# Moving the first weight conversion and the first large product in the hand-written order of an attention and feed-forward kernel

## Chip, core and metric

The kernel runs on one core of a Trainium2 chip. The metric is the device time of one execution in microseconds. Before the change three runs took 835.82, 836.37 and 837.70 us, so the median is 836.37 us.

## What is computed

The reference is windowed attention followed by a gated feed-forward layer.

```python
# q, k, v: (8 batches, 8 heads, 576 tokens, 64); x: 4608 tokens x 512
scores = (q @ k.T) / 8          # heads 0-3: the last 32 keys; heads 4-7: every 4th key of the last 128
attn   = softmax(where(mask, scores, -1e9))
x      = (attn @ v) -> 4608 x 512
h      = x @ w_in               # 512 x 2048
out    = (h * clip(h + 3, 0, 6) / 6) @ w_out   # 2048 x 512
```

## The kernel before, in words

**Attention.** The attention is cut into 48 trios; a trio is half of one batch for one of the two mask kinds. The first twelve trios are written out by hand in the table ORDER (lines 57 to 79), where each name is one step on one engine and its number is the trio. For a trio t the steps follow each other like this:

- `k`, `v` load keys with queries, and values (SP issues the transfer, L195 and L204).
- `B` is a block on PE: the mask by one product (L337), 48 score products of 64x32 (L227), and between them 48 value products (L237) of an older trio. FOLLOW says which one: block 2 carries the values of trio 0, 3 of 1, 4 of 2, 5 of 3, 7 of 5, 8 of 6, 9 of 7, 10 of 8, 11 of 9. `V` is a block with values alone.
- `R` is the maximum on DVE (L264), `S` the subtraction on DVE (L268), `X` the exponent on ACT (L291).
- `E` is the transposition on PE (L354, three products), `CA` its copy to SBUF on ACT (L367). The values' products of the trio need `CA`.
- `Z` divides by the sums on DVE (L312, L313, L315), `Y` transposes on PE (L354), `CX` copies on ACT (L371).
- `XH` rounds the tokens to the high part on ACT (L447), `XL` makes the low part on DVE (L453).

**Weights.** `w` loads one 512 KB piece of the weights (L484). It is split into a high and a low part by `Q` and `U` on ACT (L503, L499), `s`, `j` and `a` on DVE (L507, L513, L520), `h` on ACT (L523) and `l` on DVE (L529). Even pieces are w_in, odd ones w_out.

**Feed-forward.** `G` is a large product on PE, twelve matmuls of 128x384 (L545 to L547). `RE` on ACT (L553), `T` on DVE (L556), `GH` on ACT (L560) and `GL` on DVE (L564) apply the gate and split the result. `H` is the second product, nine matmuls of 128x512 (L595 to L597). After ORDER ends, a planner (`_in_time`) sets the order of all later work; it does not read ORDER.

**What sets the order.** Every engine runs its steps strictly in the order in which ORDER names them, and so does SP with the transfers. A name such as `w0@R1` means that the issue of w0 also waits until R1 is done. A step that waits therefore holds everything behind it on its engine. PE writes to two pools of PSUM banks: `ps_h` with two banks for `G`, and `ps_a` with six for all else, taken in turn.

The loop that reads the table:

```python
for name in ORDER.split():
    name, _, behind = name.partition("@")
    kind = name.rstrip("0123456789")
    issued[name] = first_operations[kind](int(name[len(kind) :]))
    if behind:
        tc.add_manual_dep(issued[name].ins, issued[behind].ins.name, ...)
```

Of the kernel before, what the change touches and what calls it, by code (L numbers as in the profile page):

```python
# [54 lines left out]

FOLLOW = {2: 0, 3: 1, 4: 2, 5: 3, 7: 5, 8: 6, 9: 7, 10: 8, 11: 9}
ORDER = """
k0 M0 M1 k1 k2 v0 k3 v1 B0 k4 v2 R0 S0 B1 X0 R1 E0 S1 w0@R1 CA0 X1 k6@X1 B2 Z0 R2 E1 CA1 Y0 k5@CA1 B3 S2 CX0 XH0 v3@S2
X2 XL0 v4@XL0 Q0 U0 E2 s0 Z1 CA2 B4 R3 j0 S3 w2@j0 a0 X3 v5@a0 h0 Y1 Z2 B6 CX1 XH1 R4 Y2 R6 E3 CX2 XL1 k7@CX2 CA3 S6
XH2 B5 S4 X6 w4@XH2 XL2 X4 Q2 l0 E6 U2 Z3 E4 v6@E6 CA6 R5 CA4 Y3 k8@CA6 s2 V4 CX3 S5 XH3 j2 X5 XL3 Q4 E5 Z4 U4 CA5 a2  # L60
Y4 B7 s4 CX4 w6@a2 j4 h2 XH4 l2 k9@j4 B8 Z5 R7 v7@R7 Y5 XL4 CX5 Z6 G0 XH5 S7 Q6 w7@Q6 R8 X7 w1@X7 XL5 Y6 U6 S8 E7 G1
CX6 a4 k10@a4 CA7 s6 v8@CA7 XH6 j6 X8 h4 XL6 B9 w5@G1 RE0 a6 RE1 l4 h6 k11@RE1 T0 E8 Q7 Z7 G2 CA8 GH0 R9 Q1 v9@GH0 GL0
U1 S9 U7 Y7 T1 B10 X9 s1 CX7 l6 GH1 v10@CX7 j1 XH7 E9 G3 R10 RE2 CA9 XL7 Q5 S10 U5 Z8 B11 X10 RE3 a1 GL1 h1 E10 T2 Y8
CA10 Z9 CX8 V10 GH2 R11 XH8 Y9 l1 CX9 Z10 H0 XH9 XL8 XL9 w3@XL8 S11 Y10 G8 GL2 CX10 w16@S11 w13@S11 T3 X11 s5 XH10 s7
GH3 XL10 E11 RE8 GL3 G6 CA11 j5 U3 w28@CA11 T8 Q3 a5 GH8 G10 j7 RE6 w11@GH8 h5 GL8 U16 T6 l5 Q16 Q13 G4 s16 GH6 a7
RE10 Q28 j16 v11@a7 h7 T10 H2 w8@j16 Q11 a16 U28 l7 h16 s3 H3 s28 GH10 GL6 l16 RE4 j3 Q8 w30@RE4 V11 U8 T4 GL10 GH4
G20 w17@U8 Z11 GL4 w9@Z11 a3 Y11 s8 RE20 G13 j28 CX11 h3 T20 XH11 j8 Q30 H4 XL11 U30 l3 w29@Q30 GH20 a8 Q17 a28 U17 H1
GL20 RE13 s17 h8 T13 Q9 j17 GH13 H8 U9 l8 w31@GH20 h28 GL13 Q31 a17 U31 G12 s9 l28 h17 Q29 j9 U29 l17 w14@GL20 G25 Q14
a9 RE12 s31 h9 s30 T12 U14 H20 l9 RE25 s14 GH12 T25 GL12 G5 w15@T25 j14 GH25 j31 GL25 a14 H13 RE5 a31 h14 T5 Q15 l14
U15 H12 j30 GH5 h31 s15 GL5 j15 G18 l31 w23@j14 Q23 a15 a30 h15 G11 s29 RE18 l15 h30 T18 l30 w18@U15 GH18 H10 j29 RE11  # L70
GL18 T11 a29 Q18 G27 GH11 U18 GL11 h29 s18 H18 l29 w19@T18 Q19 RE27 j18 U19 T27 a18 GH27 H25 s19 h18 GL27 l18 w10@Q18
Q10 U10 j19 H11 U11 s10 a19 s11 h19 j10 G22 l19 w12@a19 j11 a10 G15 RE22 a11 h10 T22 h11 l10 GH22 H6 l11 w20@j10 Q12
RE15 GL22 Q20 T15 U20 G14 GH15 s20 U12 GL15 j20 U13 s12 H22 RE14 a20 T14 h20 s13 GH14 l20 w21@l11 G7 Q21 GL14 U21 j13
j12 G24 a13 RE7 a12 h13 T7 h12 l13 w22@l20 H14 GH7 RE24 l12 GL7 T24 G17 s21 Q22 j21 GH24 U22 GL24 a21 U23 G16 RE17 s22
s23 h21 T17 j22 GH17 G9 l21 w24@l12 Q24 a22 U24 j23 h22 H24 s24 l22 j24 w25@l22 a23 H15 RE16 GL17 h23 a24 RE9 T16 h24
l23 G26 GH16 T9 Q25 GL16 U25 l24 w27@GH16 GH9 s25 G19 j25 a25 H17 h25 Q27 l25 H16 RE26 GL9 w26@H17 k12 k13 v12 v13 M2
RE19 T26 T19 G21 GH26 GH19 Q26 H9 U26 s26 U27 j26 H7 RE21 GL26 a26 T21 h26 GL19 H5 GH21 l26 GL21 s27 j27 G23 a27 h27
H21 l27 RE23 T23 GH23 H19 GL23 H23
"""


# [1466 lines left out]
```

## Time and profile before

| what | value |
|---|---|
| median of three runs | 836.37 us |
| the profiled execution's own time | 839.36 us |
| its span, first to last instruction | 837.5 us |
| PE busy in the span | 825.6 us |
| DVE busy | 646.5 us |
| ACT busy | 574.0 us |
| mean granted PE clock | 0.990 |

The profiled execution took 2.99 us longer than the median, and 1.9 us of it lie outside the span. Times in the traces count from the start of the span. A view by windows gives for each stretch of time how long each engine was busy, how many instructions it ran (x), and the granted clock of PE, where 1.00 is full speed. A timeline row gives start and duration, the engine (PEld is the weight load that goes with a PE product), the line, the tiles, and in brackets the idle time before it and what ended that. Matmuls overlap, so their durations are longer than the distance from one start to the next.

### The profile page before, as it was taken

The page shows a single profiled execution, that of the slowest core. Times are in us where ns is not written, and L with a number is a line of the kernel's source. Part 1 is how long each engine was busy: PE and PEld are TensorE (multiplying, and loading weights), DVE is VectorE, ACT ScalarE, POOL GpSimd, SP SyncE. Part 2 cuts the span into 40 slices and gives each one's busy share as a digit, 9 for nine tenths or more (in the row PEclk, how much of TensorE's full clock was granted, in tenths as well). Part 3 has the DMA queues.
Part 4 walks back from the last instruction along what each step waited for, and adds up shares of the span by engine and source line. Part 5 has one row for each costly group of instructions (what it writes and reads, how often), then busy time and mean ns, then how long its engine had stood idle before and what let it go on. Part 6 is the DMA issues. An engine that isn't in the chain of part 4 may idle for free.

```text
span 837.5 us, 22133 instructions
## 1 busy us (share of the span) xinstructions
PE 825.6 (99%) x8756; PEld 777.4 (93%) x8756; DVE 646.5 (77%) x1313; ACT 574.0 (69%) x1400; POOL 55.5 (7%) x114
## 2 busy tenths in 40 slices
PE   6999999999999999999999999999999999999998
PEld 4788999898888888999999999999999999999998
DVE  4899997646777988898898677888686798445983
ACT  3688775334799885799975698855698755455552
POOL 0000000011122212000300001000001000000000
PEclk9699999999999999999999999999999999999999
DMA  7668433242778999899997798886788866996381
GB/s 287 195 214 272 126 102 114 92 171 93 247 237 270 295 356 352 297 387 394 389 329 266 262 324 306 315 298 238 281 300 309 273 230 227 335 367 222 131 295 58
DMA packets 115783, 214.70 MB, mean 256 GB/s; under 512 B 7520, under 2 KB 40288, under 8 KB 115680
## 3 DMA queue, kind: packets, MB, share of 16 engines
q1 hardware_dynamic: 115680, 213.29, 73.3%
q8 instruction: 69, 1.13, 0.5%
q14 instruction: 34, 0.28, 0.1%
HBM read 174.47 MB, written 38.80 MB: 255 GB/s over the span
## 4 chain that ended last, share of the span: by engine, by line
PE 97%; DMA 1%; DVE 1%; ACT 0%; issue 0%; SPq 0%
PE ps_o L745 28%; PE ps_x L754 10%; PE ps_x L756 9%; PE ps_x L755 9%; PE ps_h L545 6%; PE ps_h L546 5%; PE ps_h L547 5%; PE ps_o L595 5%; PE ps_o L597 5%; PE ps_o L596 5%; PE ps_b L245 2%; PE ps_b L227 1%; PE ps_a L227 1%; PE ps_a L245 1%; PE ps_a L237 1%; PE ps_a L354 1%
## 5 line engine op out<-in xcount | busy, mean ns | idle before, releaser
L745 PE MATMUL ps_o<-gh,ring 128*128 128x384 f32 x896 | 230.8, 334 | 0.0
L745 PEld LDWEIGHTS ps_o<-gh,ring 128*128 128x128 f32 x896 | 162.0, 188 | 0.0
L745 PE MATMUL ps_o<-gl,ring 128*128 128x384 f32 x448 | 149.7, 334 | 0.0
L1208 DVE TENSOR_TENSOR gl<-g,gh 128x384 fp32r<-128x384 f32 x224 | 116.2, 553 | 27.9 <-ACT gh L1204 26.5
L1204 ACT CAST gh<-g 128x384 fp32r<-128x384 f32 x224 | 104.3, 513 | 31.2 <-PE ps_o L745 23.6
L754 PE MATMUL ps_x<-x,ring 128*128 128x384 f32 x256 | 88.4, 345 | 0.0
L545 PE MATMUL ps_h<-x,wi 128*128 128x384 f32 x256 | 88.0, 344 | 0.0
L546 PE MATMUL ps_h<-x,wi 128*128 128x384 f32 x256 | 86.2, 337 | 0.0
L755 PE MATMUL ps_x<-x,ring 128*128 128x384 f32 x256 | 86.1, 336 | 0.0
L756 PE MATMUL ps_x<-x,ring 128*128 128x384 f32 x256 | 86.1, 336 | 0.0
L547 PE MATMUL ps_h<-x,wi 128*128 128x384 f32 x256 | 86.1, 336 | 0.0
L745 PEld LDWEIGHTS ps_o<-gl,ring 128*128 128x128 f32 x448 | 84.1, 188 | 0.1
L595 PE MATMUL ps_o<-wo,gh 128*128 128x512 f32 x192 | 74.9, 390 | 0.0
L596 PE MATMUL ps_o<-wo,gh 128*128 128x512 f32 x192 | 74.7, 389 | 0.0
L597 PE MATMUL ps_o<-wo,gl 128*128 128x512 f32 x192 | 74.7, 389 | 0.0
L553 ACT ACTIVATE t<-ps_h,three 128x384 f32<-128x384 f32 x64 | 37.1, 582 | 50.6 <-PE ps_h L547 50.5
L756 PE MATMUL ps_x<-cell,ring 128*128 128x384 f32 x192 | 64.9, 338 | 0.0
L755 PE MATMUL ps_x<-cell,ring 128*128 128x384 f32 x192 | 64.7, 337 | 0.0
L754 PE MATMUL ps_x<-cell,ring 128*128 128x384 f32 x192 | 64.7, 337 | 0.0
L1173 DVE TENSOR_TENSOR g<-g 128x768 f32<-128x768 f32 x64 | 60.8, 951 | 0.0
L556 DVE SCALAR_TENSOR_TENSOR t<-t,ps_h 128x384 f32<-128x384 f32 x64 | 35.1, 550 | 28.6 <-ACT t L553 27.9
L1058 DVE TENSOR_TENSOR s<-ps_x,s 128x384 f32<-128x384 f32 x64 | 35.3, 552 | 25.3 <-ACT s L1051 24.6
(112 smaller groups left out, 1767.6 us busy)
## 6 DMA issues: line engine op xcount, KB each, us to landing
ring<-sums SPq DMA_DIRECT2D x112, 512.0 KB, 8.3
ring<-rights SPq DMA_DIRECT2D x112, 512.0 KB, 7.2
st<-in_w SPq DMA_DIRECT2D x32, 512.0 KB, 4.3
kq<-in_qk SPq DMA_DIRECT2D x39, 416.0 KB, 5.1
v<-in_v SPq DMA_DIRECT2D x39, 390.0 KB, 5.6
sums<-wi SPq DMA_DIRECT2D x24, 256.0 KB, 6.5
rights<-wo SPq DMA_DIRECT2D x24, 256.0 KB, 5.4
out<-o SPq DMA_DIRECT2D x15, 384.0 KB, 2.8
```

What stands on the lines that cost most here:

```text
L545: nc.tensor.matmul(ph, lhsT=wt(f, 0)[:, ks], rhs=a, start=(kt == 0), stop=False)
L546: nc.tensor.matmul(ph, lhsT=wt(f, 0)[:, ks], rhs=b, start=False, stop=False)
L547: ins = nc.tensor.matmul(ph, lhsT=wt(f, 1)[:, ks], rhs=a, start=False, stop=(kt == NK - 1))
L595: nc.tensor.matmul(po[c][tt], lhsT=gh[:, rows], rhs=wt(f, 2), start=first, stop=False)
L596: nc.tensor.matmul(po[c][tt], lhsT=gh[:, rows], rhs=wt(f, 3), start=False, stop=False)
L597: return nc.tensor.matmul(po[c][tt], lhsT=gl[:, rows], rhs=wt(f, 2), start=False, stop=(f == NF - 1))
L745: nc.tensor.matmul(banks[part][:, :CH], lhsT=right[:, a, cols], rhs=x, start=(start and not i), stop=(i == 2), skip_group_check=True)
L754: nc.tensor.matmul(bank, lhsT=tile_[:, 0, ks], rhs=h[:, kt], start=(start and kt == 0), stop=False, skip_group_check=True)
L755: nc.tensor.matmul(bank, lhsT=tile_[:, 0, ks], rhs=l[:, kt], start=False, stop=False, skip_group_check=True)
L756: nc.tensor.matmul(bank, lhsT=tile_[:, 1, ks], rhs=h[:, kt], start=False, stop=(kt == 1), skip_group_check=True)
L1204: nc.scalar.copy(two[0], gated_tile(g, q, k))
L1208: nc.vector.tensor_tensor(out=two[1], in0=gated_tile(g, q, k), in1=two[0].bitcast(F32), op=ALU.subtract)
```

## The change

Only the table ORDER changes. Its first 18 names and its last 417 of 588 stay as they are; the 153 between are the same names in another order, and 13 of the transfers among them wait for another step than before. No instruction is added or taken away.

```diff
-k0 M0 M1 k1 k2 v0 k3 v1 B0 k4 v2 R0 S0 B1 X0 R1 E0 S1 w0@R1 CA0 X1 k6@X1 B2 Z0 R2 E1 CA1 Y0 k5@CA1 B3 S2 CX0 XH0 v3@S2
-X2 XL0 v4@XL0 Q0 U0 E2 s0 Z1 CA2 B4 R3 j0 S3 w2@j0 a0 X3 v5@a0 h0 Y1 Z2 B6 CX1 XH1 R4 Y2 R6 E3 CX2 XL1 k7@CX2 CA3 S6
...
-Y4 B7 s4 CX4 w6@a2 j4 h2 XH4 l2 k9@j4 B8 Z5 R7 v7@R7 Y5 XL4 CX5 Z6 G0 XH5 S7 Q6 w7@Q6 R8 X7 w1@X7 XL5 Y6 U6 S8 E7 G1
...
+k0 M0 M1 k1 k2 v0 k3 v1 B0 k4 v2 R0 S0 B1 X0 R1 E0 S1 CA0 X1 w0@X1 B2 Z0 R2 E1 CA1 k6@CA1 Y0 B3 S2 CX0 k5@S2 XH0 X2
+XL0 v3@XL0 E2 CA2 Z1 R3 v4@R3 B4 S3 Q0 X3 U0 s0 j0 w2@j0 Y1 CX1 a0 v5@a0 h0 Z2 B6 XH1 R4 Y2 R6 E3 CX2 XL1 k7@CX2 CA3
...
+k9@Z4 U4 CA5 a2 Y4 s4 j4 B7 CX4 h2 XH4 l2 XL4 w6@XL4 G0 a4 R7 h4 S7 RE0 X7 Z5 B8 l4 E7 v8@X7 Y5 CA7 T0 CX5 G1 R8 XH5
+Q6 XL5 S8 X8 Z6 Y6 CX6 U6 k10@XL5 w7@Q6 B9 RE1 XH6 s6 E8 T1 j6 CA8 XL6 w1@Z6 a6 G2 h6 R9 Q7 S9 l6 w5@G2 X9 Z7 k11@a6
```

There are two places. On ACT, near the first weight conversion, the rows are Q0 (L503), U0 (L499), CA2 (L367), X3 (L291), h0 (L523) and CX1 (L371); the difference reads:

```order
-L503 ACTIVATE va<-st 128x512
-L499 ACTIVATE va<-st 128x512
-L367 COPY a<-ps_a 128x384
-L291 ACTIVATE e<-e 128x384
-L523 CAST wi<-va 128x512
-L371 COPY xf<-ps_a 128x6x2x32
+L367 COPY a<-ps_a 128x384
+L503 ACTIVATE va<-st 128x512
+L291 ACTIVATE e<-e 128x384
+L499 ACTIVATE va<-st 128x512
+L371 COPY xf<-ps_a 128x6x2x32
+L523 CAST wi<-va 128x512
```

CA2 now stands ahead of Q0, and X3 between Q0 and U0; on DVE, R3 and S3 likewise stand ahead of s0 and j0.

On PE, behind block 7, the first large product G0 (L545 to L547) now comes at once; these are its first rows:

```order
 L237 MATMUL ps_a<-first,a 32x65
 L227 MATMUL ps_a<-first 32x64
+L545 MATMUL ps_h<-x_78,wi 128x384
+L546 MATMUL ps_h<-x_84,wi 128x384
+L547 MATMUL ps_h<-x_78,wi 128x384
```

PE's order there was block 7, block 8, Y5, G0, Y6, E7, G1, block 9; it is now block 7, G0, block 8, E7, Y5, G1, Y6, block 9.

On DVE, the followers of block 8 stood like this before: Z6 (three rows), S7, R8, XL5 (L453), S8, then a4, s6, j6 of the weights:

```order
L312 TENSOR_SCALAR z<-ps_a 128x6
L313 RECIPROCAL z<-z 128x6
L315 TENSOR_TENSOR x<-ps_a,z 128x384
L268 TENSOR_TENSOR e<-ps_a,mx 128x384
L264 TENSOR_REDUCE mx<-ps_a 128x6
L453 TENSOR_TENSOR x_86<-xf,x_80 128x2x192
L268 TENSOR_TENSOR e<-ps_a,mx 128x384
L520 ISA va<-va 128x1024
L507 TENSOR_SCALAR va<-va 128x512
L513 SCALAR_TENSOR_TENSOR va<-st,va 128x512
```

Now R8, XL5 and S8 stand ahead of Z6, and T1 (L556) stands between s6 and j6:

```order
L264 TENSOR_REDUCE mx<-ps_a 128x6
L453 TENSOR_TENSOR x_86<-xf,x_80 128x2x192
L268 TENSOR_TENSOR e<-ps_a,mx 128x384
L312 TENSOR_SCALAR z<-ps_a 128x6
L313 RECIPROCAL z<-z 128x6
L315 TENSOR_TENSOR x<-ps_a,z 128x384
L507 TENSOR_SCALAR va<-va 128x512
L556 SCALAR_TENSOR_TENSOR t<-t,ps_h 128x384
L513 SCALAR_TENSOR_TENSOR va<-st,va 128x512
```

Z6 moved behind XL5. Further on, DVE's order is XL6, a6, R9, S9, l6, Z7, GL0, s1, j1, where it was XL6, a6, l4, T0, Z7, R9, GL0, S9, T1, s1, l6, j1.

More of the change, by code (lines that the diff above doesn't have):

```diff
@@ L57 @@
 ORDER = """
-k0 M0 M1 k1 k2 v0 k3 v1 B0 k4 v2 R0 S0 B1 X0 R1 E0 S1 w0@R1 CA0 X1 k6@X1 B2 Z0 R2 E1 CA1 Y0 k5@CA1 B3 S2 CX0 XH0 v3@S2
-X2 XL0 v4@XL0 Q0 U0 E2 s0 Z1 CA2 B4 R3 j0 S3 w2@j0 a0 X3 v5@a0 h0 Y1 Z2 B6 CX1 XH1 R4 Y2 R6 E3 CX2 XL1 k7@CX2 CA3 S6
-XH2 B5 S4 X6 w4@XH2 XL2 X4 Q2 l0 E6 U2 Z3 E4 v6@E6 CA6 R5 CA4 Y3 k8@CA6 s2 V4 CX3 S5 XH3 j2 X5 XL3 Q4 E5 Z4 U4 CA5 a2
-Y4 B7 s4 CX4 w6@a2 j4 h2 XH4 l2 k9@j4 B8 Z5 R7 v7@R7 Y5 XL4 CX5 Z6 G0 XH5 S7 Q6 w7@Q6 R8 X7 w1@X7 XL5 Y6 U6 S8 E7 G1
-CX6 a4 k10@a4 CA7 s6 v8@CA7 XH6 j6 X8 h4 XL6 B9 w5@G1 RE0 a6 RE1 l4 h6 k11@RE1 T0 E8 Q7 Z7 G2 CA8 GH0 R9 Q1 v9@GH0 GL0
@@ L63 @@
[L63 to L77, printed above, removed]
@@ L78 @@
-H21 l27 RE23 T23 GH23 H19 GL23 H23
+k0 M0 M1 k1 k2 v0 k3 v1 B0 k4 v2 R0 S0 B1 X0 R1 E0 S1 CA0 X1 w0@X1 B2 Z0 R2 E1 CA1 k6@CA1 Y0 B3 S2 CX0 k5@S2 XH0 X2
+XL0 v3@XL0 E2 CA2 Z1 R3 v4@R3 B4 S3 Q0 X3 U0 s0 j0 w2@j0 Y1 CX1 a0 v5@a0 h0 Z2 B6 XH1 R4 Y2 R6 E3 CX2 XL1 k7@CX2 CA3
+S6 XH2 B5 S4 X6 w4@XH2 XL2 X4 Q2 l0 E6 U2 Z3 E4 v6@E6 CA6 R5 CA4 Y3 k8@CA6 s2 V4 CX3 S5 XH3 j2 X5 XL3 v7@XL3 Q4 E5 Z4
+k9@Z4 U4 CA5 a2 Y4 s4 j4 B7 CX4 h2 XH4 l2 XL4 w6@XL4 G0 a4 R7 h4 S7 RE0 X7 Z5 B8 l4 E7 v8@X7 Y5 CA7 T0 CX5 G1 R8 XH5
@@ new lines @@
+Q6 XL5 S8 X8 Z6 Y6 CX6 U6 k10@XL5 w7@Q6 B9 RE1 XH6 s6 E8 T1 j6 CA8 XL6 w1@Z6 a6 G2 h6 R9 Q7 S9 l6 w5@G2 X9 Z7 k11@a6
+Y7 Q1 CX7 B10 U1 U7 GH0 v9@GH0 GL0 s1 GH1 v10@CX7 j1 XH7 E9 G3 R10 RE2 CA9 XL7 Q5 S10 U5 Z8 B11 X10 RE3 a1 GL1 h1 E10
+T2 Y8 CA10 Z9 CX8 V10 GH2 R11 XH8 Y9 l1 CX9 Z10 H0 XH9 XL8 XL9 w3@XL8 S11 Y10 G8 GL2 CX10 w16@S11 w13@S11 T3 X11 s5
+XH10 s7 GH3 XL10 E11 RE8 GL3 G6 CA11 j5 U3 w28@CA11 T8 Q3 a5 GH8 G10 j7 RE6 w11@GH8 h5 GL8 U16 T6 l5 Q16 Q13 G4 s16
+GH6 a7 RE10 Q28 j16 v11@a7 h7 T10 H2 w8@j16 Q11 a16 U28 l7 h16 s3 H3 s28 GH10 GL6 l16 RE4 j3 Q8 w30@RE4 V11 U8 T4 GL10
@@ new lines @@
+GH4 G20 w17@U8 Z11 GL4 w9@Z11 a3 Y11 s8 RE20 G13 j28 CX11 h3 T20 XH11 j8 Q30 H4 XL11 U30 l3 w29@Q30 GH20 a8 Q17 a28
+U17 H1 GL20 RE13 s17 h8 T13 Q9 j17 GH13 H8 U9 l8 w31@GH20 h28 GL13 Q31 a17 U31 G12 s9 l28 h17 Q29 j9 U29 l17 w14@GL20
+G25 Q14 a9 RE12 s31 h9 s30 T12 U14 H20 l9 RE25 s14 GH12 T25 GL12 G5 w15@T25 j14 GH25 j31 GL25 a14 H13 RE5 a31 h14 T5
+Q15 l14 U15 H12 j30 GH5 h31 s15 GL5 j15 G18 l31 w23@j14 Q23 a15 a30 h15 G11 s29 RE18 l15 h30 T18 l30 w18@U15 GH18 H10
+j29 RE11 GL18 T11 a29 Q18 G27 GH11 U18 GL11 h29 s18 H18 l29 w19@T18 Q19 RE27 j18 U19 T27 a18 GH27 H25 s19 h18 GL27 l18
@@ new lines @@
+w10@Q18 Q10 U10 j19 H11 U11 s10 a19 s11 h19 j10 G22 l19 w12@a19 j11 a10 G15 RE22 a11 h10 T22 h11 l10 GH22 H6 l11
+w20@j10 Q12 RE15 GL22 Q20 T15 U20 G14 GH15 s20 U12 GL15 j20 U13 s12 H22 RE14 a20 T14 h20 s13 GH14 l20 w21@l11 G7 Q21
+GL14 U21 j13 j12 G24 a13 RE7 a12 h13 T7 h12 l13 w22@l20 H14 GH7 RE24 l12 GL7 T24 G17 s21 Q22 j21 GH24 U22 GL24 a21 U23
+G16 RE17 s22 s23 h21 T17 j22 GH17 G9 l21 w24@l12 Q24 a22 U24 j23 h22 H24 s24 l22 j24 w25@l22 a23 H15 RE16 GL17 h23 a24
+RE9 T16 h24 l23 G26 GH16 T9 Q25 GL16 U25 l24 w27@GH16 GH9 s25 G19 j25 a25 H17 h25 Q27 l25 H16 RE26 GL9 w26@H17 k12 k13
@@ L79 @@
+v12 v13 M2 RE19 T26 T19 G21 GH26 GH19 Q26 H9 U26 s26 U27 j26 H7 RE21 GL26 a26 T21 h26 GL19 H5 GH21 l26 GL21 s27 j27
+G23 a27 h27 H21 l27 RE23 T23 GH23 H19 GL23 H23
 """
```

## The prediction

> **What bounds the kernel now.** First the page: span, PE's share, and the chain that ended last.
>
> ```profile
> span 837.5 us, 22133 instructions
> PE 825.6 (99%) x8756; PEld 777.4 (93%) x8756; DVE 646.5 (77%) x1313; ACT 574.0 (69%) x1400; POOL 55.5 (7%) x114
> q8 instruction: 69, 1.13, 0.5%
> PE 97%; DMA 1%; DVE 1%; ACT 0%; issue 0%; SPq 0%
> ```
>
> PE bounds it: it idles for 11.9 us in all. The view by windows says when.
>
> ```profile
> 58.40:837.00 778.60, 775.56 (x7512) 738.48 (x7510) 604.29 (x1210) 538.05 (x1319) 54.88 (x108) 1.00 0.74 258
> ```
>
> From 58.4 us on PE idles for 3.0 us in 778.6, at full clock. The change ends before that point, and all later work keeps its order, so whatever first moves the second product H0 (56.04 us) moves the end by as much. The question is how long PE needs to reach H0. Two things delay it there. One is the clock, in windows of 3.41 us, at whose edges it changes:
>
> ```profile
> 7.97:11.38 3.41, 2.49 (x103) 1.74 (x101) 1.61 (x6) 1.38 (x3) 0.00 (x0) 1.00 1.01 391
> 14.79:18.21 3.42, 0.62 (x36) 0.47 (x36) 1.56 (x5) 1.58 (x3) 0.00 (x0) 1.00 0.79 297
> 28.45:31.86 3.41, 1.90 (x55) 1.28 (x54) 3.32 (x10) 3.38 (x9) 0.00 (x0) 1.00 0.84 268
> 31.86:35.27 3.41, 3.41 (x101) 2.31 (x101) 2.29 (x6) 1.91 (x6) 0.00 (x0) 0.50 0.62 193
> 35.27:38.69 3.42, 3.42 (x102) 3.18 (x102) 3.24 (x10) 0.40 (x1) 0.00 (x0) 0.50 0.68 218
> ```
>
> The columns are length, busy time of PE, PEld, DVE, ACT and POOL, clock, DMA share, GB/s. After a window with 0.62 us of PE work, and after one with 1.90, the clock is half; after 2.49 it stayed whole. The other is the wait in block 4, in the chain that ended last (start, length, what):
>
> ```profile
> 8.06 7.26 DMA st<-in_w
> 15.34 0.66 ACT va L503
> 16.55 0.38 ACT a L367
> 16.98 0.24 PE ps_a L237
> 17.55 1.02 issue
> ```
>
> The load of w0 ends at 15.32, Q0 (L503) waits for it, U0 and then CA2 (L367) stand behind it, and block 4's values start at 16.98. Then PE waits for another 1.02 us, and no semaphore is named. The same happened one block earlier (the other two rows are the end of E2 and block 4's mask):
>
> ```profile
> 12.79 0.21 PE L237 MATMUL ps_a<-first,a 64*32 64x65 f32 x1 [0.22 <-issue]
> 14.19 0.38 PE L354 MATMUL ps_a<-ident,e 128*128 128x128 f32 x2
> 14.51 0.33 PE L337 MATMUL ps_a<-mi 32*128 32x384 bf16 x1
> ```
>
> Between the stop that ends at 12.79 and the one that ends at 18.57 the timeline has 127 matmuls (88 of block 3, 3 transposes, 36 of block 4), with a weight load each: 254 instructions. The page's 17,512 PE instructions over its 69 instruction loads are 254 too. I read both stops as PE waiting for the next piece of its code, while the data loads fill the DMA engines (share 1.01 in the window 7.97:11.38).
>
> **First part: CA2 and R3 ahead of the conversion.** E2 ends at about 14.57, so CA2 can run at 14.65 and block 4's values start at 15.2 instead of 16.98: 1.78 us earlier. But after 36 matmuls, some 0.4 us, PE needs the same piece of code. Up to block 4's mask (14.51) nothing on PE changes, and w0 is only issued some 1.2 us later into a queue that is full anyway, so the piece should arrive at the same 18.57. Then block 4 ends where it did, the window 14.79 to 18.21 again holds some 0.6 us of PE work, and the clock halves as before. The bounds are 0 (the piece comes when it came) and 1.78 us (its wait vanishes); I take 0, since the code load is what ended last in that row. R3, S3 and Z1 come earlier, which nothing uses: PE's next steps, Y1 and block 6, stand behind block 4. The transfers of k6, k5, v3 and v4 are issued one step later each, behind a queue that still has work, for blocks that start after 20 us: nothing.
>
> The Trainium skill, "Runtime: NRT & Kernel Launch", section "Instruction fetch mechanics", has PE's code streamed in blocks of 256 instructions, the crossing "mostly hidden". The block's size agrees with the 254; the 1.02 us does not agree with hidden. By that page this part would gain the 1.78 us.
>
> **Second part: G0 ahead of block 8.** The PE rows from here on, before:
>
> ```profile
> 32.48 0.49 PE L337 MATMUL ps_a<-mi 32*128 32x384 bf16 x1
> 34.91 0.50 PE L337 MATMUL ps_a<-mi 32*128 32x384 bf16 x1
> 40.45 0.49 PE L354 MATMUL ps_a<-ident,x 128*128 128x128 f32 x3
> 41.02 0.42 PE L545 MATMUL ps_h<-x,wi 128*128 128x384 f32 x1
> 43.30 0.33 PE L337 MATMUL ps_a<-mi 32*128 32x384 bf16 x1
> 44.89 0.55 PE L354 MATMUL ps_a<-ident,e 128*128 128x128 f32 x3
> 56.04 0.47 PE L595 MATMUL ps_o<-wo,gh 128*128 128x512 f32 x1
> ```
>
> They are block 7, block 8, Y6, G1, block 9, E8 and H0. A large product takes about 2.1 us at full clock (2.28 from G1 to block 9, with the change of operand), a block 1.59 (43.30 to 44.89). DVE's and ACT's costs, each from one start to the next, come from these rows: on DVE Z7 (45.00 to 45.89: 0.89), R9, GL0, S9, T1, s1, l6, and j1 in the last:
>
> ```profile
> 45.00 0.16 DVE L312 TENSOR_SCALAR z<-ps_a 128x6 f32<-128x6 f32 x1 [0.49 <-PE ps_a L237]
> 45.89 0.55 DVE L264 TENSOR_REDUCE mx<-ps_a 128x6 f32<-128x384 f32 x1
> 46.40 0.56 DVE L564 TENSOR_TENSOR gl<-t,gh 128x384 fp32r<-128x384 f32 x1
> 46.88 0.55 DVE L268 TENSOR_TENSOR e<-ps_a,mx 128x384 f32<-128x384 f32 x1
> 47.34 0.54 DVE L556 SCALAR_TENSOR_TENSOR t<-t,ps_h 128x384 f32<-128x384 f32 x1
> 47.81 0.42 DVE L507 TENSOR_SCALAR va<-va 128x512 uint32<-128x512 uint32 x1
> 48.14 0.68 DVE L529 TENSOR_TENSOR wi<-va,wi 128x512 fp32r<-128x512 f32 x1
> 48.74 0.69 DVE L513 SCALAR_TENSOR_TENSOR va<-st,va 128x512 uint32<-128x512 uint32 x1
> ...
> 55.32 0.68 DVE L529 TENSOR_TENSOR wo<-va,wo 128x512 fp32r<-128x512 f32 x1
> ```
>
> So 0.47 us for R, S, T, GL (and XL in one piece), 0.33 for s, 0.6 for j, a, l. On ACT 0.4 for a copy or rounding, 0.5 for RE, 0.55 for U:
>
> ```profile
> 41.72 0.53 ACT L447 CAST x<-xf 128x384 fp32r<-128x384 f32 x1
> 42.13 0.54 ACT L291 ACTIVATE e<-e 128x384 f32<-128x384 f32 x1
> 43.07 1.06 ACT L553 ACTIVATE t<-ps_h,three 128x384 f32<-128x384 f32 x2
> 46.83 1.21 ACT L499 ACTIVATE va<-st 128x512 f32<-128x512 f32 x2
> ```
>
> A step on another engine starts about 0.1 us after the end of what it waits for. Step by step:
>
> 1. *To G1, no change.* G0 starts when block 7 is done, 34.95, at half clock until 38.69: 3.74 us there are 1.87 of its 2.1, so it ends at 38.9. Block 8 runs 38.9 to 40.5, now at full clock, E7 40.55, Y5 40.9, G1 41.2 to 43.3 (before 41.02 to 43.3). The half-clocked time went to G0 instead of block 8; RE0 holds ACT until 39.2, X7 follows at 39.7, in time for E7.
> 2. *Y6, +1.3 us.* Y6 needs Z6, and DVE has R8, XL5 and S8 first. XL5 waits for XH5, that for CX5, that for Y5's end at 41.4: CX5 41.5, XH5 42.0, XL5 42.55, S8 43.05, Z6 43.5 to 44.5, Y6 44.6. PE is idle from 43.3 on. DVE, ready with R8 at 41.2, stands still for 1.4 us with Z6's input (block 8, done 40.5) behind the waiting XL5.
> 3. *Y7, +2.7 us.* Block 9 runs 44.95 to 46.55, E8, G2 46.9 to 49.0; Y7 needs Z7. ACT: CX6 45.2, U6 45.6, RE1 46.15, XH6 46.65. DVE: s6 behind U6 46.3, T1 behind RE1 46.8, j6 47.25, XL6 47.85, a6 48.3, R9 48.9, S9 49.4, l6 50.0, Z7 50.6 to 51.6, Y7 51.7. T1, R9, S9 and l6 (2.0 us) are what stood behind Z7 before; the rest is the late Y6.
> 4. *H0, another 2.3 us.* Block 10 starts at 52.05. H0 needs l1, the low part of w1. DVE's GL0 now waits for GH0, which stands on ACT behind CX7 (52.3, after Y7) and U1, U7: GH0 53.8 to 54.3, GL0 54.4. From there s1, j1, R10, XL7 (0.9), S10, Z8, a1, GL1, T2, Z9, R11 take 0.33+0.6+0.47+0.9+0.47+0.89+0.6+0.47+0.47+0.89+0.47 = 6.6 after GL0's 0.47, with some 0.3 of waits: l1 at 61.7 instead of 55.32, H0 at about 62.4 instead of 56.04.
>
> Sum: +6.3 us at H0, three stops of PE of 1.3, 2.7 and some 2.3 us. Of the moved transfers, v7 and k9 come sooner than their blocks need them, and w6 (behind XL4, about 35.3) is landed long before Q6 at 42.5. The one that is close is v9, now behind GH0 at 54.3; loads of values take
>
> ```profile
> v<-in_v SPq DMA_DIRECT2D x2, 390.0 KB, 3.8
> ```
>
> so it lands at 58.1, and block 11 ends near 59.6, before Z9 would want it (60.2): hidden by DVE's queue, with 0.6 us to spare.
>
> **The clock on top.** The stop 49.0 to 51.7 leaves some 1.0 us of PE work in a window of 3.41. By the row 28.45:31.86 (1.90 us of work, then half clock) the clock halves behind it. One halved window costs nothing, since DVE holds PE up there; each further one of dense large products would cost up to 1.7. I take 0.7, from 0 to 1.7. The Trainium skill, "TensorE: Matmul & The Clock Gate", section "Why this matters for your kernels", wants no idle gap above about 3 us; by it 2.7 us would be free and the sum 6.3. The row 28.45:31.86 speaks against it.
>
> So the profiled execution, 839.36, becomes 846.4; that execution stood 3.0 us above the median, so the same 7.0 us on the median of 836.37 give **843.4 us**.
>
> **The rivals.**
>
> *The code arrives sooner, in part (+4.6).* If the piece of code comes with the block, the whole start moves up, but not by more than 1.75: s0, j0 and a0 now stand directly ahead of Z2 and wait for w0 (15.32), which holds Y2. 836.4 + 6.3 − 1.75 = 841.0. The page of the Trainium skill named above speaks for it. Against it stand the two stops 254 instructions apart.
>
> *Not slower: the start runs at full clock.* Without the stop PE has some 2.7 us of work between 14.79 and 18.21, more than the 2.49 that kept the clock. If it then stays whole past 38.69, block 7 saves 0.84 (2.43 at half, 32.48 to 34.91, against 1.59), G0 1.87, transposes some 0.4, and with the 1.75 that is 4.9 of the 6.3: 837.8 us, within 0.2%. It decides if the code comes before about 16.3. Against it also: the 1.90 us window at 28.45, whose gaps the change leaves.
>
> *More half clock.* If the stops keep the clock halved into the dense products after H0, two or three more windows cost 1.7 each: 845 to 848 us.
>
> *DVE's waits don't add up, or the order does less than it says.* If Z6 and Z7 were not held up, G0 ahead of block 8 is worth 0 and the time stays at 836.4 or slightly less. Against it: the rows of DVE's order are unambiguous.
>
> **Numbers.** Forecast 0.60 (842.7 to 844.4), partly sooner 0.15, more half clock 0.12, full clock 0.08, no stops 0.05. The range 838.0 to 847.0 leaves out the last two and the top of the third, with what is unknown of the windows' phase. A difference of 0.2% (1.7 us) is about what a measurement of this kernel can tell. Slower by over 0.2%: 0.87; within: 0.09; faster: 0.04.
>
> **What would show it.** In the new profile: block 4's first values at about 15.2, then an "issue" stop to about 18.5; G0 at 35.0, block 8 at 38.9; PE idle before Y6 and Y7, released by DVE's x (L315); DVE idle before XL5; l1 at about 61.7; H0 near 62.4; half clock in a window after 52. I am wrong if block 4 runs through without a stop and the clock is whole at 20 us, or if Y6 follows G1 without a gap.

## The result and the profile after

The changed kernel takes 841.51 us (median of six runs, 840.14 to 844.9). The kernel before took 837.04 us (median of six, 835.66 to 838.68). The ratio is 1.006, with a 95% interval of 1.0044 to 1.0077: the change costs about 4.5 us. The forecast was 843.4 us, a change of 7.0: the direction and the wide range hold, and the change is 2.5 us smaller than forecast. The profiled execution of the changed kernel is the longest of its six, with a span of 843.1 us against 837.5, so its trace shows a difference of 5.6 us where the medians show 4.5. Of the executions in the experiments below, two single ones, of 1608 and 2646 us, lie far outside all others and are left out.

The page of the changed kernel, then its view by windows; the last row is the long stretch that answers to 58.40:837.00 of before:

```profile
span 843.1 us, 22144 instructions
...
PE 825.8 (98%) x8756; PEld 775.8 (92%) x8756; DVE 647.3 (77%) x1313; ACT 575.0 (68%) x1400; POOL 55.6 (7%) x114
...
PE 93%; DVE 3%; DMA 1%; ACT 1%; issue 1%; SPq 0%; DVEq 0%
```

```profile
15.78:19.19 3.41, 1.04 (x79) 0.89 (x63) 2.17 (x5) 1.24 (x3) 0.00 (x0) 1.00 0.77 259
19.19:22.60 3.41, 3.41 (x63) 2.51 (x56) 2.08 (x7) 1.41 (x3) 0.00 (x0) 0.50 0.78 254
...
26.02:29.43 3.41, 1.73 (x54) 1.40 (x54) 3.38 (x10) 3.08 (x9) 0.00 (x0) 1.00 0.90 285
...
32.84:36.26 3.42, 3.42 (x61) 3.25 (x44) 3.32 (x10) 1.02 (x3) 0.00 (x0) 0.50 0.61 172
36.26:39.67 3.41, 3.41 (x111) 2.89 (x109) 2.06 (x4) 1.30 (x3) 0.00 (x0) 1.00 0.35 111
39.67:43.08 3.41, 2.30 (x14) 2.01 (x14) 1.85 (x5) 2.17 (x5) 0.00 (x0) 1.00 0.46 138
...
46.50:49.91 3.41, 1.15 (x8) 0.83 (x7) 3.15 (x8) 2.19 (x4) 0.00 (x0) 1.00 0.46 129
49.91:53.32 3.41, 3.41 (x102) 2.58 (x103) 0.57 (x2) 2.69 (x8) 0.00 (x0) 0.50 0.50 195
...
62.86:841.80 778.94, 775.82 (x7512) 738.14 (x7510) 604.95 (x1211) 538.76 (x1319) 54.98 (x108) 1.00 0.75 258
```

PE's busy time, in which halved work counts with its longer time, is the same within 0.2 us (825.8 against 825.6), so in this pair of executions the difference is idle time: one halved window more behind Y7 stands against two fewer behind block 4. From 62.86 us on PE idles for 3.1 us, where it idled for 3.0 before. Nearly all of that lies behind its last product (2.4 us here, all 3.0 before); the other 0.74 us are one stop, shown further down. Ahead of 62.86 us lie three windows with little PE work, 1.04, 1.73 and 1.15 us, and behind each the clock is half (0.50). The window with 2.30 us keeps the whole clock. The window 46.50:49.91 and the halved one behind it are new.

Block 4 in the chain that ended last, and PE's rows from G0 on in the timeline:

```profile
14.89 0.49 ACT a L367
15.38 0.04 issue
15.42 0.24 PE ps_a L237
...
15.99 2.37 issue
```

```profile
33.77 0.69 PE L545 MATMUL ps_h<-x,wi 128*128 128x384 f32 x1
...
37.18 0.33 PE L337 MATMUL ps_a<-mi 32*128 32x384 bf16 x1
...
39.41 0.42 PE L545 MATMUL ps_h<-x,wi 128*128 128x384 f32 x1
...
42.86 0.52 PE L354 MATMUL ps_a<-ident,x 128*128 128x128 f32 x3 [1.11 <-DVE x L315]
...
49.81 0.85 PE L354 MATMUL ps_a<-ident,x 128*128 128x128 f32 x3 [2.26 <-DVE x L315]
...
58.79 0.94 PE L237 MATMUL ps_a<-v,a 64*32 64x65 f32 x48 [0.60 <-ACT a L367]
...
59.97 0.48 PE L595 MATMUL ps_o<-wo,gh 128*128 128x512 f32 x1
...
60.65 0.50 PE L596 MATMUL ps_o<-wo,gh 128*128 128x512 f32 x1 [0.20 <-DVE wo L529]
```

Block 4's values start at 15.42 and not at 16.98, and PE then waits for its code until 18.36, nearly as late as before (18.57): 2.37 us instead of 1.02. G0 follows block 7 at 33.77, block 8 comes at 37.18, G1 at 39.41. Then Y6 (42.86) and Y7 (49.81) are late by 1.11 and 2.26 us, both times for DVE's division (L315). H0 starts at 59.97, 3.93 us later than before. DVE's rows in the same stretch say why:

```profile
40.80 0.56 DVE L453 TENSOR_TENSOR x<-xf,x 128x384 fp32r<-128x384 f32 x1 [1.34 <-ACT x L447]
...
41.74 0.15 DVE L312 TENSOR_SCALAR z<-ps_a 128x6 f32<-128x6 f32 x1
...
44.51 0.43 DVE L507 TENSOR_SCALAR va<-va 128x512 uint32<-128x512 uint32 x1 [1.80 <-ACT va L499]
...
48.78 0.16 DVE L312 TENSOR_SCALAR z<-ps_a 128x6 f32<-128x6 f32 x1
...
52.75 0.56 DVE L564 TENSOR_TENSOR gl<-t,gh 128x384 fp32r<-128x384 f32 x1 [2.99 <-ACT gh L560]
...
59.91 0.68 DVE L529 TENSOR_TENSOR wo<-va,wo 128x512 fp32r<-128x512 f32 x1
```

DVE stands still for 1.34 us at XL5 (40.80) while Z6's input is ready; Z6 runs only at 41.74. From s6 (44.51) DVE works without a pause to Z7 (48.78), with T1, R9, S9 and l6 among the steps in between. Before GL0 it stands still again for 2.99 us. H0's second row (60.65) then waits 0.20 us for l1, the row at 59.91. In the profiled execution another 1.1 us go between 62.9 and 77 us, 0.74 of them at V11, whose values wait for their load. The traces of the second part alone and of the kernel with GH0 early, further down, have no wait there, so it is not a fixed cost of the change:

```profile
76.96 0.94 PE L237 MATMUL ps_a<-v,a 64*32 64x65 f32 x48 [0.74 <-DMA v<-in_v]
```

### The profile page after: what moved, and what is told of

Same layout as the page of the kernel before. It is cut to its first block, busy times and chain, and to the rows that moved or that the text cites. A ratio compares the mean times of both kernels' runs of the same rounds, so it can differ in the third digit from the quotient of the medians.

```text
span 843.1 us, 22144 instructions
## 1 busy us (share of the span) xinstructions
PE 825.8 (98%) x8756; PEld 775.8 (92%) x8756; DVE 647.3 (77%) x1313; ACT 575.0 (68%) x1400; POOL 55.6 (7%) x114
## 3 DMA queue, kind: packets, MB, share of 16 engines
q8 instruction: 69, 1.13, 0.5%
## 4 chain that ended last, share of the span: by engine, by line
PE 93%; DVE 3%; DMA 1%; ACT 1%; issue 1%; SPq 0%; DVEq 0%
PE ps_o L745 28%; PE ps_x L754 10%; PE ps_x L756 9%; PE ps_x L755 9%; PE ps_h L545 5%; PE ps_o L595 5%; PE ps_o L596 5%; PE ps_o L597 5%; PE ps_h L546 5%; PE ps_h L547 5%; PE ps_b L245 2%; PE ps_b L227 1%; PE ps_a L245 1%; PE ps_a L227 1%; PE ps_a L354 1%
## 5 line engine op out<-in xcount | busy, mean ns | idle before, releaser
L545 PE MATMUL ps_h<-x,wi 128*128 128x384 f32 x256 | 88.6, 346 | 0.0
L547 PE MATMUL ps_h<-x,wi 128*128 128x384 f32 x256 | 86.4, 338 | 0.0
L556 DVE SCALAR_TENSOR_TENSOR t<-t,ps_h 128x384 f32<-128x384 f32 x64 | 35.2, 551 | 29.3 <-ACT t L553 28.7
```

Of the source, the lines that this page charges most:

```text
L545: nc.tensor.matmul(ph, lhsT=wt(f, 0)[:, ks], rhs=a, start=(kt == 0), stop=False)
L547: ins = nc.tensor.matmul(ph, lhsT=wt(f, 1)[:, ks], rhs=a, start=False, stop=(kt == NK - 1))
```

## The experiments

Three theories stood against each other. A: the order of G0's followers on DVE and ACT carries the loss. B: the first part carries it, by later loads and a later conversion. C: G0 ahead of block 8 costs by itself. The kernels are the kernel before or the changed one with other rows in ORDER; one has other warm-up products too. A diff shows the stretch of ORDER that matters, cut at both ends. They ran in four groups, each beside its own runs of the kernel before (medians 837.27, 836.94, 837.08 and 837.0 us).

**The first part alone.** The change's table up to h0, then that of before. Against the kernel before, with w0, k6 and k5, which stand ahead of this stretch, issued later as in the change:

```diff
-XL0 v4@XL0 Q0 U0 E2 s0 Z1 CA2 B4 R3 j0 S3 w2@j0 a0 X3 v5@a0 h0 Y1 Z2 B6 CX1
+XL0 v3@XL0 E2 CA2 Z1 R3 v4@R3 B4 S3 Q0 X3 U0 s0 j0 w2@j0 Y1 CX1 a0 v5@a0 h0 Z2 B6
```

> Only the first part of the change: the table as before from XL3 on, as changed up to there. Theory A (the followers of G0 carry the loss): 0 to -1 us against before, and block 4 still stops for its code, from about 15.8 to 18.4 us of the span. Theory B (the first part, with its later loads and later conversion, carries the loss): +3 to +4.5 us. Theory C (G0 ahead of block 8 costs by itself, whatever follows): as A.

Measured: 836.47 us against 837.27, ratio 0.9991 (0.9979 to 1.0003). Its timeline shows the same stop at the same place as the changed kernel's:

```profile
18.16 0.26 PE L227 MATMUL ps_a<-first 64*32 64x64 f32 x1 [2.26 <-issue]
```

Block 4 begins its values sooner, and the wait for code takes the time back. Theory B falls: this part costs nothing that can be measured. Whether it gains some tenths stays open.

**The second part alone.** The changed kernel with the rows above, and the issues of w0, k6 and k5, put back:

```diff
-XL0 v3@XL0 E2 CA2 Z1 R3 v4@R3 B4 S3 Q0 X3 U0 s0 j0 w2@j0 Y1 CX1 a0 v5@a0 h0 Z2 B6
+XL0 v4@XL0 Q0 U0 E2 s0 Z1 CA2 B4 R3 j0 S3 w2@j0 a0 X3 v5@a0 h0 Y1 Z2 B6 CX1
```

> Only the second part of the change: the table as before up to XL3, as changed from there. Theory A: +4.5 to +6.3 us, with PE idle before Y6 (about 1.3 us), before Y7 (about 2.7 us), and DVE idle before GL0 (about 3 us). Theory B: 0 to +1 us. Theory C: +4.5 us or more.

Measured: 842.27 against 837.27, ratio 1.0058 (1.0040 to 1.0077). The whole loss is here, within the interval. The stops are those of the changed kernel, though this execution ran at full clock from 13.15 to 30.2 us and so came to Y6 2.3 us sooner:

```profile
40.55 0.52 PE L354 MATMUL ps_a<-ident,x 128*128 128x128 f32 x3 [1.13 <-DVE x L315]
47.51 0.90 PE L354 MATMUL ps_a<-ident,x 128*128 128x128 f32 x3 [2.27 <-DVE x L315]
```

**The followers put back.** The changed kernel with Z6 ahead of R8, Z7 ahead of R9, and GH0 ahead of U1:

```diff
-G1 R8 XH5 Q6 XL5 S8 X8 Z6 Y6
+G1 Z6 R8 XH5 Q6 XL5 S8 X8 Y6
-h6 R9 Q7 S9 l6 w5@G2 X9 Z7 k11@a6 Y7 Q1 CX7 B10 U1 U7 GH0 v9@GH0 GL0
+h6 Z7 R9 Q7 S9 l6 w5@G2 X9 k11@a6 Y7 Q1 CX7 B10 GH0 U1 U7 v9@GH0 GL0
```

> The changed table with three steps put ahead of what waits: Z6 ahead of R8, Z7 ahead of R9 on DVE, GH0 ahead of U1 on ACT. Theory A: about half of the loss goes, +2 to +2.8 us against before; the stop before Y6 shrinks to under 0.3 us and that before Y7 by about 1.5 us. Theory B: unchanged, +4.5. Theory C: unchanged, +4.5.

Measured: 839.64 against 837.27, ratio 1.0030 (1.0018 to 1.0043). About half of the loss comes back. PE's timeline behind block 7:

```profile
45.42 0.55 PE L354 MATMUL ps_a<-ident,x 128*128 128x128 f32 x3 [0.78 <-DVE x L315]
52.01 0.21 PE L237 MATMUL ps_a<-v,a 64*32 64x65 f32 x1 [1.60 <-DMA v<-in_v]
```

The stop before Y6 is gone and that before Y7 is 0.78 us. A new one stands in block 11, for the values v9; in the changed kernel PE comes to that block later and does not wait for them.

**G0 alone.** The kernel before with only XL4 and G0 ahead of block 8:

```diff
-l2 k9@j4 B8 Z5 R7 v7@R7 Y5 XL4 CX5 Z6 G0 XH5
+l2 XL4 k9@j4 G0 B8 Z5 R7 v7@R7 Y5 CX5 Z6 XH5
```

> The table of before with only G0 put ahead of block 8, and XL4 ahead of G0, which needs it. Theory A: +2.0 to +2.5 us, from one new stop of PE before E7 of about 2.4 us (block 8 ends later, and Z6 stands on DVE ahead of S7, whose exponent E7 needs), and no stop before Y7. Theory B: 0. Theory C: +4.5 us.

Measured: 839.46 against 837.27, ratio 1.0030 (1.0013 to 1.0046).

```profile
40.91 0.52 PE L354 MATMUL ps_a<-ident,x 128*128 128x128 f32 x3 [0.69 <-DVE x L315]
42.31 0.55 PE L354 MATMUL ps_a<-ident,e 128*128 128x128 f32 x3 [0.88 <-ACT e L291]
```

G0 had lain between Y5 and Y6 and given DVE its time for Z6. Moved ahead, it leaves that place empty, and PE waits for Z6 (0.69 us, before Y6) and then for X7 (0.88 us, before E7). So C holds for about half of the loss. Theory A had named the same size, 2.0 to 2.5 us, but from one stop of 2.4 us before E7: its number came by luck. The prediction had this move at nothing.

**The followers alone.** The kernel before with DVE's order alone changed: Z6 behind R8, XL5 and S8, Z7 behind R9, S9, T1 and l6, and GL0 behind Z7. PE, ACT and the transfers keep their order.

```diff
-Y5 XL4 CX5 Z6 G0 XH5 S7 Q6 w7@Q6 R8 X7 w1@X7 XL5 Y6 U6 S8 E7
+Y5 XL4 CX5 G0 XH5 S7 Q6 w7@Q6 R8 X7 w1@X7 XL5 S8 Z6 Y6 U6 E7
-T0 E8 Q7 Z7 G2 CA8 GH0 R9 Q1 v9@GH0 GL0 U1 S9 U7 Y7 T1 B10 X9 s1 CX7 l6 GH1 v10@CX7
+T0 E8 Q7 G2 CA8 GH0 R9 Q1 v9@GH0 U1 S9 U7 T1 l6 Z7 GL0 Y7 B10 X9 s1 CX7 GH1 v10@CX7
```

> The kernel before, with only DVE's order changed as the change has it behind block 8: Z6 behind S7, R8, XL5 and S8, and Z7 behind R9, S9, T1 and l6; PE, ACT and the transfers as before, so G0 still lies between Y5 and Y6. Theory 1 (DVE's order carries half of the loss whatever PE does, the half that was given back when Z6 and Z7 went to their old places): stops before Y6 of some 0.8 us and before Y7 of some 2 us, and 2.2 us slower than before, near 839.3 us. Theory 2 (the order costs only where G0 is no longer there to fill PE): G0's 2.1 us cover Y6, Y7 waits less than 1 us, and the time stays within 0.8 us of before.

Measured: 838.92 against 837.0, ratio 1.0018 (1.0005 to 1.0031).

```profile
37.99 0.52 PE L354 MATMUL ps_a<-ident,x 128*128 128x128 f32 x3 [1.13 <-DVE x L315]
45.73 0.55 PE L354 MATMUL ps_a<-ident,x 128*128 128x128 f32 x3 [0.63 <-DVE x L315]
```

DVE's order costs even with G0 in its old place: G0 and the stop of 1.13 us together make the wait for Z6. Theory 1 has the total, but other sizes (1.13 and 0.63 us instead of 0.8 and 2). This and G0 alone, 1.9 and 2.2 us, add up to 4.1 of the 4.5 us; each is known to about 1.1 to 1.4 us only. In both profiled executions the clock stays whole behind the stops (1.00 from 44 to 60 us with G0 alone, and from 45.70 to 54.30, that is from Y7 to H0, in this kernel).

**The gate's rounding early.** The changed kernel with GH0 (and with it the issue of v9) right behind h6, which takes DVE's 2.99 us before GL0 away:

```diff
-h6 R9 Q7 S9 l6 w5@G2 X9 Z7 k11@a6 Y7 Q1 CX7 B10 U1 U7 GH0 v9@GH0 GL0
+h6 GH0 R9 Q7 S9 l6 w5@G2 X9 Z7 k11@a6 Y7 Q1 CX7 B10 U1 U7 v9@GH0 GL0
```

> The changed kernel with one edit: the rounding GH0 stands on ACT right behind h6, ahead of Q7, Q1, CX7 and U1, where ACT idled; v9, which waits for GH0, is issued sooner with it. It undoes step 4 of the prediction alone (DVE's 2.99 us of standing before GL0). Theory 1 (that wait is a cost of its own, as step 4 had it: DVE's chain from GL0 to l1 sets H0): l1 some 1.6 us earlier, since s1 then waits for U1 behind CX7 instead, and the time 1.6 us below the changed kernel, near 839.9 us. Theory 2 (the wait lies under PE's own stop before Y7 and PE is level with DVE by block 11): only the 0.60 us before V10 and the 0.2 us in H0 can go, 840.7 us.

> The same kernel as the one with GH0 right behind h6, whose profiled execution was not usable: one look at its trace. DVE does not stand still before GL0 for more than 0.2 us; the stop before Y7 stays at some 2.2 us; block 11's values wait less than 0.3 us for v9; the wait before V10 is gone or moves to s1, which waits for U1 behind CX7.

Measured: ratio 1.0053 (1.0035 to 1.0070) against 837.08, so 4.4 us, where the changed kernel has 4.5. The second kernel is the same one, run for its trace. It has the stops of 1.11 and 2.26 us before Y6 and Y7 unchanged, and from Y7 (48.78) to H0 (60.10) PE waits at most 0.24 us at a time. DVE's row for s1, then PE's windows around Y7:

```profile
50.80 0.43 DVE L507 TENSOR_SCALAR va<-va 128x512 uint32<-128x512 uint32 x1 [1.61 <-ACT va L499]
```

```profile
45.30:48.71 3.41, 1.22 (x7) 0.90 (x6) 3.31 (x9) 2.11 (x5) 0.00 (x0) 1.00 0.45 105
48.71:52.12 3.41, 3.34 (x101) 2.51 (x102) 1.59 (x4) 3.00 (x7) 0.00 (x0) 0.50 0.97 354
52.12:55.53 3.41, 3.41 (x12) 3.41 (x13) 3.29 (x10) 2.82 (x7) 0.00 (x0) 0.50 0.27 100
```

Taking GL0's wait away alone gives back nothing that can be measured. Theory 1, which was step 4 of the prediction, wanted 839.9 us, a ratio of 1.0034, just below the interval; theory 2's 840.7 us lies inside it. In this trace DVE has a new wait in place of the old one (1.61 us at s1, for U1 on ACT), and what PE needs from Y7 to H0 is set by the clock, half for two windows behind the stop, and not by DVE. That is not so in every execution: two others of this kernel had a granted clock of 1.000 over their whole span and took 840.76 and 840.89 us. Five executions of the kernel before with 1.000 took 834.79 to 837.50, median 836.51. So this kernel is some 4.3 us slower without any half clock too.

**All of the followers put back, v9 early.** The kernel of the followers with GH0 right behind h6 too:

```diff
-h6 Z7 R9 Q7 S9 l6 w5@G2 X9 k11@a6 Y7 Q1 CX7 B10 GH0 U1 U7 v9@GH0 GL0
+h6 GH0 Z7 R9 Q7 S9 l6 w5@G2 X9 k11@a6 Y7 Q1 CX7 B10 U1 U7 v9@GH0 GL0
```

> The earlier kernel with Z6 and Z7 in their old places, with GH0 also behind h6 as in the run beside it, so that v9 is issued some 3 us sooner than there. Theory 1 (the 1.6 us wait for v9 in block 11 holds what that kernel had over the one before, 2.4 us): 838.0 us. Theory 2 (DVE's l1 sets H0 all the same, and it comes only by GL0's 0.5 us sooner): 839.1 us. If neither moves it, 839.6, the rest lies ahead of block 10.

Measured: 839.92 against 837.08, ratio 1.0034 (1.0019 to 1.0048). Theory 1's gain of 1.6 us did not come; theory 2's 0.5 us is too small to tell here. Block 11 still waits for v9, although it is issued at 45.42 instead of 48.82:

```profile
51.84 0.21 PE L237 MATMUL ps_a<-v,a 64*32 64x65 f32 x1 [1.58 <-DMA v<-in_v]
```

```profile
L204 SPq DMA_DIRECT2D v<-in_v x2: 328/360/392, 45.4 to 47.8; - x2
...
DMA to landing us min/median/max: 4.9/5.6/6.3
```

The two loads of values take 4.9 and 6.3 us to land here; in the trace of the kernel with the followers put back they take 3.1 and 4.5, and PE gets v9 at 51.84 here and at 52.01 there. The weights w1 and w5 and the keys k11 are issued just ahead of v9. The earlier issue alone did not bring the data sooner.

**Is the stop in block 4 code?** The first part alone, with 20 warm-up matmuls of 204 columns instead of 8 of 512: as much PE time, and 24 more instructions (12 matmuls with a weight load each).

```diff
-WARM = 8
+WARM = 20
-        nc.tensor.matmul(idle, lhsT=zeros[:, :P], rhs=zeros[:, P : P + 512], start=True, stop=True)
+        nc.tensor.matmul(idle[:, :204], lhsT=zeros[:, :P], rhs=zeros[:, P : P + 204], start=True, stop=True)
```

> As the first part alone, with 20 warm-up matmuls of 204 columns in place of 8 of 512: 24 more PE instructions ahead of block 0, about the same time. If the stop in block 4 is PE waiting for its next 256 instructions, it moves 12 matmuls forward, from behind 36 to behind 24 matmuls of block 4, and that of block 3 moves out of that block into Y0, E1 or the end of block 2. If it is a wait for data or a bank, it stays behind the 36th matmul. No difference in the time of more than 1 us is expected.

Measured: 837.35 against 836.94, ratio 1.0003 (0.9983 to 1.0022). PE's work between the start of block 4's values and the stop, in the windows view of the first part alone and then of this kernel:

```profile
15.00:18.10 3.10, 0.59 (x36) 0.47 (x36) 1.89 (x5) 2.01 (x4) 0.00 (x0) 0.95 0.88 309
```

```profile
15.40:17.25 1.85, 0.47 (x23) 0.31 (x24) 1.21 (x3) 1.34 (x4) 0.00 (x0) 1.00 0.92 307
```

The stop lies behind 36 weight loads in the one and behind 24 in the other. It kept its running number among PE's instructions and moved 12 products ahead in the block. No data or semaphore of block 4 would do that, so the stop is PE waiting for its next 254 instructions.

**Does the code come late because of the loads?** The first part alone, with four loads issued later:

```diff
-CA1 k6@CA1 Y0 B3 S2 CX0 k5@S2 XH0 X2 XL0 v3@XL0 E2 CA2 Z1 R3 v4@R3 B4 S3 Q0
+CA1 Y0 B3 S2 CX0 XH0 X2 XL0 k6@XL0 E2 CA2 Z1 k5@Z1 R3 v3@R3 B4 S3 v4@S3 Q0
```

> As the first part alone, with the loads k6, k5, v3, v4 issued only behind XL0, Z1, R3, S3 (14.0 to 16.5 us), so that about 2.5 fewer data loads are queued when the code for block 4 is asked for. If the code queues behind the data, the stop in block 4 ends 0.7 to 1.4 us sooner than in the first part alone, and the time falls by 0.5 to 2 us against it; at most 1.75 us can be gained ahead of Y2 beside the clock. If the code does not queue behind data, the stop ends at 18.4 us as before and the time is the same.

Measured: 836.83 against 836.94, ratio 0.9995 (0.9980 to 1.0010).

```profile
15.90 0.21 PE L227 MATMUL ps_a<-first 64*32 64x64 f32 x1 [0.49 <-issue]
```

```profile
19.83 0.44 PE L354 MATMUL ps_a<-ident,x 128*128 128x128 f32 x2 [1.43 <-DVE x L315]
```

The stop is short, 0.49 us, and ends at 15.90, and PE then waits for 1.43 us before Y2, because Z2 stands behind the first conversion on DVE. That is the cap that the prediction named for sooner code. The cause of the short stop is not settled, though: the kernel with the followers put back has the changed kernel's loads there, and its stop was 0.60 us in its one profiled execution. How late the code comes varies from one execution to the next.

## Why the prediction was right, and where it was too large

The sum was 1.3 + 2.7 + 2.3 us for three stops and 0.7 for the clock. The two stops before Y6 and Y7 came where and why it said, and make 3.4 of the 4.5 us measured. For step 4 and the clock together it had 3.0 us, and 1.1 are left: that is where it was too large. The narrow range to which it gave 0.60, 842.7 to 844.4, was missed.

**First part, taken at 0: right.** The first part alone is at 0.9991 (0.9979 to 1.0003). The values started at 15.42 (15.2 forecast), and the stop ended at 18.36 (18.5). That it was code was inferred from the count 254; the shifted stop shows it. In other executions the stop was only 0.49 to 0.63 us, so the code does not always come that late; what that would be worth was not measured.

**Step 1, no change to G1: right for the time, wrong as a reason.** G1 was not late. But "G0 ahead of block 8 is worth 0" fails: G0 alone costs 2.2 us, because it no longer fills PE while DVE divides. The changed kernel has G1 in that place ahead of Y6, and none is left for the next gap; how much of the stops before Y6 and Y7 comes from that and how much from DVE's order, only the two separate runs say (2.2 and 1.9 us).

**Step 2, +1.3 us: 1.11 us.** XL5 waited 1.34 us (1.4 forecast) with Z6 behind it.

**Step 3, +2.7 us: 2.26 us.** From s6 to Z7 the trace has 4.27 us where the working had 4.3. Steps 2 and 3 together are 3.4 of the 4.0 us forecast.

**Step 4, another 2.3 us: too large.** Its chain is there: from Y7 to l1 10.1 us, forecast 10.0. (By the working's own rows the step is 2.0 us and not 2.3: 51.7 to 62.4 is 10.7 us, against 8.66 before.) What it left out is that PE is not idle meanwhile. These rows are the stretch from Y7 to H0, before and after:

```profile
47.38:56.04 8.66, 8.42 (x271) 7.03 (x269) 8.26 (x22) 7.79 (x21) 0.00 (x0) 1.00 0.46 161
```

```profile
49.81:59.97 10.16, 9.56 (x270) 7.89 (x270) 7.05 (x19) 8.48 (x22) 0.00 (x0) 0.83 0.42 150
```

The stretch is 1.50 us longer, not 2.0. PE's stops make 0.36 of it (0.60 us before V10, 0.24 before the change); the other 1.14 are PE's work taking longer (9.56 us instead of 8.42), at half clock for one window. DVE and PE then reach H0 together: l1 starts at 59.91, and H0's second row waits 0.20 us for it. So in this execution the two limits lie side by side and do not add up, and taking DVE's wait alone away, as in the kernel with GH0 early, brings nothing that can be measured.

**The clock, +0.7 us: the mechanism came, its share is not shown.** The prediction let one halved window cost nothing, since DVE would hold PE up, and that fits this trace, where l1 comes no sooner than PE. The table has PE's larger new stops between block 7 and H0, the time from Y7 to H0 and the halved windows in that stretch, all from one profiled execution of each kernel, and the loss from the medians or the ratio. The waits before V10 are left out, and so is a stop of 0.76 us inside G0 in the fourth kernel, for which no semaphore is named:

| kernel | new stops behind block 7, us | sum | Y7 to H0, us | halved windows | slower by, us |
|---|---|---|---|---|---|
| followers alone | 1.13, 0.63 | 1.8 | 8.54 | 0 | 1.9 |
| G0 alone | 0.69, 0.88 | 1.6 | 9.26 | 0 | 2.2 |
| followers put back | 0.78, 1.60 | 2.4 | 10.88 | 0 | 2.4 |
| followers put back, v9 early | 0.77, 1.58 | 2.4 | 11.19 | 1 | 2.8 |
| changed | 1.11, 2.26 | 3.4 | 10.16 | 1 | 4.5 |
| changed, GH0 early | 1.11, 2.26 | 3.4 | 11.32 | 2 | 4.4 |
| second part alone | 1.13, 2.27 | 3.4 | 11.25 | 2 | 5.0 |

In the first three rows, with the whole clock behind Y7, the stops give the time to within 0.6 us (the two kernels with 1.6 us for v9 have that stop between Y7 and H0). The fourth has a halved window and 0.4 us more than these stops, less than the one left out. The three kernels with the long stop before Y7 have a window with 1.15 to 1.38 us of PE work there and half clock behind it in these traces, and are 1.0 to 1.6 us slower than the two stops say.

It is tempting to call that rest the clock. Between executions of one kernel the clock does count: the two of the changed kernel with a mean granted clock of 0.991 and 0.992 took 844.9 and 843.72 us, the four with 0.995 to 0.997 took 840.14 to 841.63. But the kernel with GH0 early is 4.3 us slower at a clock of 1.000 as well, so half clock is not needed for a loss of that size, though two executions cannot tell 4.3 from 3.4. The changed kernel's trace, for its part, has 0.36 us more before V10, 0.20 in H0 and 0.74 before V11, which the table leaves out. What the remaining 1.0 to 1.6 us are is open: DVE's chain and the clock lie in the same stretch, and no trace has the long stop with the whole clock.

**The rivals.** "The code arrives sooner, in part" had 841.0 us, closer to 841.51 than the forecast, but not for its reason: the stop ended at 18.36 in the trace, and the second part alone, at 5.0 us, is already below the 7.0 made for it. "More half clock" has its mechanism in three traces, but in the changed kernel's it lies beside DVE's chain and not on top of it. "Full clock" and "no stops" did not come. The clock was half for one window behind block 4 in the changed kernel and for three before, and block 7 came 1.15 us sooner in this execution. This was in no term, and it is chance: the first part alone, with the same rows and loads there, had three halved windows in its trace.

## What to carry to other kernels

A large product placed ahead of a chain is no free gain: look at what it was filling, and who fills that gap now. Where an engine takes its steps strictly in order, a step that waits for another engine (here XL5) should not stand ahead of one whose input is ready and for which the busiest engine waits (here Z6). When stops follow each other, add only what the bounding engine loses: a second engine's wait in the same stretch may lie under it. And a trace is one execution: before a rest is put down to the clock, look at executions that had the whole clock.

## What the runs showed of the hardware

- PE's code comes in pieces of 254 instructions here, and PE waits between two pieces early in the kernel: 0.49 to 2.37 us in eleven traces, at the same running instruction in each (1.02 us before the change). The length differs between executions with the same loads up to there (0.60 and 2.37 us, and 0.63 to 2.25 in the four traces that start like the kernel before).
- The clock was halved behind windows of 3.41 us with 1.04, 1.15 and 1.73 us of PE work in the changed kernel, and kept behind one with 2.30. No single gap in the second of these was longer than 2.26 us. PE's work in the window alone does not decide it: a window with 1.85 us kept the clock (39.81:43.23 with G0 alone) and one with 2.15 lost it (19.69:23.10 in the kernel with the shifted code). Before the change three halved windows stood in a row; the first two held less than a full window of work, and the third was filled, after which the clock was whole:

```profile
18.21:21.62 3.41, 3.05 (x84) 2.22 (x87) 3.19 (x8) 1.88 (x4) 0.00 (x0) 0.50 0.44 158
21.62:25.04 3.42, 3.28 (x71) 2.38 (x71) 1.96 (x4) 1.58 (x5) 0.00 (x0) 0.50 0.40 134
25.04:28.45 3.41, 3.41 (x102) 3.24 (x85) 3.17 (x9) 2.91 (x9) 0.00 (x0) 0.50 0.77 215
```

  In the changed kernel the filled windows 19.19:22.60, 32.84:36.26 and 49.91:53.32 are also the last at half clock, and in the kernel with GH0 early the window with 3.34 us of work is followed by another half one and the filled one by a whole one. The filled window 31.86:35.27 of before is an exception: it was followed by another half one. What restores the clock is therefore not settled.
